# A fused linear-attention and gated-FFN kernel: its last stage put into a written order on all engines, small operands in PSUM, the first tiles' sums spread over the rounds before, and the output weights' splits gathered in one pass

## The chip, the cores and the metric

The kernel runs on one core of a Trainium2 chip. The metric is device time in microseconds (us). TensorE (PE) multiplies matrices from SBUF into PSUM, VectorE (DVE) and ScalarE (ACT) work on SBUF and PSUM, GpSimd (POOL) on SBUF, and SyncE (SP) issues every DMA. Each engine takes its instructions strictly in the order in which they were put into its queue; where an instruction waits for a semaphore, all behind it wait too.

## The reference

Sizes: S = 2048 tokens, D = 1024, 32 heads of 32, FF = 3584, all float32.

```python
xn = _layernorm(x, axis=-1)
# A: hedgehog linear attention, per head
pq, pk = q @ w_phi, k @ w_phi
phi_q = concat([softmax(pq), softmax(-pq)]); phi_k = concat([softmax(pk), softmax(-pk)])
kv = phi_k^T v ; z = sum(phi_k)
o = (phi_q kv) / (phi_q z + 1e-6)
s = o @ wo
# B: SwiGLU
g = _silu((_silu(xn @ w1) * (xn @ w3)) @ w2)
return x + s * g
```

## The kernel before

Each float32 operand of the large products is split into a high and a low float32r part (`split`: one ACT cast, one DVE subtraction), and a product is three passes over the parts (`PASSES`). The large products also use seven instead of eight block products (`ORDER`, `TURN`; the names A11, S2, T3 and so on are the sums and blocks of that scheme).

The program runs through five stretches. First layer norm and FFN's two up-products (L556), to 1184 us of the trace. Then three passes over eight pairs of token tiles (L639): pass c = 0 and c = 1 make keys and values (`heads`), pass c = 2 makes queries (`queries`) and stores for each of the 16 tiles `e`, two halves of 128x1024 exponentials, in DRAM. Between the products of the first two passes `split_wo` prepares the output weights `wo`: one block for each of the 16 pairs, loaded at step 0, split at step 3, stored at step 5 (L787 to L798). Each pair has seven steps, one per block product.

Then "down" (L913), from 1677 us: 7 blocks `kb` times 8 pairs `i`, a round per pair. A round is seven groups of six matmuls in the order S1, A11, S3, A12, S4, S2, A22 (`TURN`), three of them for the new pair (A11, A12, S2), the other four for the pair before. The groups of a pair share PSUM banks, so that S3 goes into the bank only after DVE has read S2 out of it, A22 after S3, S4 after S1. DVE adds the results into `acc` (L925); for A11, ACT copies (L922) and POOL adds (L923). In the last block (kb = 6) a finished pair is passed through SiLU (`gate`, L866) and stored to `g_d`, its `acc` buffers come free, and the loads of `e`, of `zb` (the sums z, spread to all partitions) and the output weights `wos` come in. The last, extra round has only S1, S3, S4, A22.

The last stage works tile by tile, 16 of them. `scales` turns e into weighted features: POOL multiplies e by zb into `ez` (L884), DVE sums e (L885) and ez (L887) over each head, six small operations of 128x32 give the factors `by` (L891 to L896), and both halves of e are multiplied by them, half 0 on DVE and half 1 on POOL (L899). `attend` transposes e on PE (`pt`, L1002), ACT copies it out (`et`, L1004), PE multiplies by kv (`po`, L1011), and `po` is split into `oT` (ACT L90, DVE L91). `output` multiplies oT by the output weights (`pm`, L99, 24 matmuls for each half of the columns), DVE multiplies by the gate (L1026), POOL adds x (L1027; DVE in the last tile), SP stores.

What sets the order: outside of `in_order(...)` a scheduler orders all engines' instructions by its own estimate; inside, the named engines keep the order in which the program writes them. Before the change, the last stage had SP, ACT, DVE and POOL in order for the extra round only, and SP alone for the first two tiles; for the rest the scheduler decided. `halves` and `output` are generators that interleave one tile's attention with the output product of the tile before.

Of the kernel before, what the change touches and what calls it, by code (L numbers as in the profile page):

```python
# [28 lines left out]
def tile_kernel(ctx: ExitStack, tc: tile.TileContext, x, wkT, wqT, wv, wphi, wo, w1, w3, w2, out):  # L29
# [757 lines left out]
    wso = []  # L787

    def split_wo(c, k, j):
        if j == 0:  # L790
            wso.append(work.tile([P, 512], F, name="wsr", tag="w"))
            nc.sync.dma_start(wso[-1], wo[k * P:(k + 1) * P, c * 512:(c + 1) * 512])
        elif j == 3:
            wso.append(quad("wso").rearrange("p u k t -> p u (k t)"))
            split(wso[1][:, 0], wso[1][:, 1], wso[0])
        elif j == 5:
            nc.sync.dma_start(wo_d[c][k], wso[1].bitcast(F))
            wso.clear()  # L798
# [8 lines left out]
    for c in range(3):  # L807
# [49 lines left out]
    wos, es = {}, {}  # L857
# [11 lines left out]
    E_TAGS = (0, 4, 1, 5, 2, 6)  # L869

    def load_e(i):

        two = []
        for c in range(2):
            two.append(accp.tile([P, 1024], F, name="e", tag=f"acc{E_TAGS[(2 * i + c) % 6]}"))
            nc.sync.dma_start(two[c], e_d[i][c])
        return two

    def scales(e):

        sums = small.tile([P, 2, 2, 16, 2], F, name="sums")
        for c in range(2):
            ez = accp.tile([P, 1024], F, name="ez", tag="accE", bufs=3)
            nc.gpsimd.tensor_mul(ez, e[c], zb[c])  # L884
            nc.vector.tensor_reduce(sums[:, 0, c].rearrange("p h s -> p (h s)"), e[c].rearrange("p (h f) -> p h f", f=DH),  # L885
                                    axis=AX.X, op=OP.add)
            nc.vector.tensor_reduce(sums[:, 1, c].rearrange("p h s -> p (h s)"), ez.rearrange("p (h f) -> p h f", f=DH),  # L887
                                    axis=AX.X, op=OP.add)
        by = small.tile([P, 2, 16, 2], F, name="by")
        t = small.tile([P, 2, 2, 16], F, name="rho")  # L890
        nc.vector.reciprocal(t[:, 0], sums[:, 0, :, :, 1])  # L891
        nc.vector.tensor_mul(t[:, 0], sums[:, 0, :, :, 0], t[:, 0])
        nc.vector.tensor_mul(t[:, 1], sums[:, 1, :, :, 1], t[:, 0])  # L893
        nc.vector.tensor_add(t[:, 1], t[:, 1], sums[:, 1, :, :, 0])  # L894
        nc.vector.reciprocal(by[:, :, :, 0], t[:, 1])  # L895
        nc.vector.tensor_mul(by[:, :, :, 1], by[:, :, :, 0], t[:, 0])  # L896
        for c, eng in enumerate((nc.vector, nc.gpsimd)):
            e3 = e[c].rearrange("p (h f) -> p h f", f=DH)
            eng.tensor_mul(e3, e3, by[:, c].rearrange("p h s -> p (h s)").unsqueeze(2).to_broadcast([P, H, DH]))  # L899
        return e  # L900
# [31 lines left out]
    for r, new in enumerate(steps):  # L932
# [32 lines left out]
        if end:  # L965
# [5 lines left out]
            if i == 3:  # L971
# [3 lines left out]
                es[0] = load_e(0)  # L975
            if i == 4:
# [12 lines left out]
    ps = pool("ps4", 3, space=PSUM)  # L989

    gate(*pairs[-1])
    in_order(ENG.SP)

    def attend(c, e):


        po = ps.tile([P, 2, 512], F, name="po", tag="po", bufs=1)
        ets = []
        for q in range(2):
            pt = ps.tile([P, 4, P], F, name="pt2", tag="tr", bufs=3)  # L1000
            for g in range(4):
                nc.tensor.transpose(pt[:, g, :], e[:, (4 * q + g) * P:(4 * q + g + 1) * P], ident)  # L1002
            et = work.tile([P, 4, P], F, name="et", tag="w")
            nc.scalar.copy(et, pt)  # L1004
            ets.append(et)
        yield
        for q, et in enumerate(ets):
            for g in range(4):
                for hh in range(2):
                    sl = slice(64 * hh, 64 * hh + 64)  # L1010
                    nc.tensor.matmul(po[32 * g:32 * g + 32, hh, q * P:(q + 1) * P], kvu[sl, G * c + 4 * q + g], et[sl, g],  # L1011
                                     start=True, stop=True, skip_group_check=True)
        oT = quad("oT")
        o4 = oT.rearrange("p u (h q) t -> p u h q t", q=2)
        split(o4[:, 0], o4[:, 1], po[:, :, :2 * P].rearrange("p h (q t) -> p h q t", t=P))
        yield oT

    def output(i, oT):
        for c in range(2):
            cs = slice(c * 512, c * 512 + 512)  # L1020
            gx = accp.tile([P, 2, 512], F, name="gx", tag="accZ", bufs=3)
            nc.sync.dma_start(gx[:, 0], g_d[i][:, cs])
            nc.sync.dma_start(gx[:, 1], x[i * P:(i + 1) * P, cs])
            for p in project([t[:, :, k] for t in oT for k in range(4)], lambda k, a: wos[c, k][:, a]):
                yield
# [69 lines left out]
```

## Time and profile before

| what | value |
|---|---|
| three runs | median 2488.62 us (2486.26 to 2493.84) |
| the profiled execution, its own time | 2484.93 us |
| its span, first to last instruction | 2483.1 us |
| granted TensorE clock, mean | 0.995 |
| PE busy | 96% of the span |
| DVE, ACT, POOL busy | 69%, 36%, 30% |
| DMA | mean 236 GB/s |

In rows of the timeline the columns are start (us from the span's start), duration (us), engine, source line, operation, output<-inputs, shapes, count, and in brackets how long the engine had sat idle before it and what released it. PE's matmul durations overlap: the distance between the starts of two groups is what counts (2.72 us for 12 matmuls of 128x512). Rows of the waits list total us, times and the longest. Rows of one line's instructions give min/median/max in ns.

### The profile page before, as it was taken

What the parts mean: (1) busy time and instruction counts of PE and PEld (TensorE: products, weight loads), DVE (VectorE), ACT (ScalarE), POOL (GpSimd) and SP (SyncE); (2) the same over time, 40 slices, a digit from 0 to 9 for tenths busy, and PEclk for the clock granted to TensorE, in tenths of its full rate; (3) what the DMA queues carried; (4) which work ended last, traced back from release to release, by engine and by line L of the source; (5) the groups of instructions that cost most, each with busy time, mean ns of one, the idle gap of its engine ahead of it and who ended that gap; (6) DMA issues with size and microseconds to landing.
All of it is one profiled execution on the core that took longest, in us unless ns stands there. A gap on an engine that the chain in (4) does not pass through costs nothing. (4 is left out here: it accounts for less than half of the span.)

```text
span 2483.1 us, 35840 instructions
## 1 busy us (share of the span) xinstructions
PE 2388.2 (96%) x13552; PEld 1950.1 (79%) x13552; DVE 1704.0 (69%) x2465; ACT 900.8 (36%) x1564; POOL 735.4 (30%) x513
## 2 busy tenths in 40 slices
PE   5999999999999999999999999899999999988999
PEld 5888877788777887878788788787888888866777
DVE  8656777774567777774566666566678878897773
ACT  6444544443344444542222122234322222332221
POOL 1233455553355555551000000000011111146662
PEclk9999999999999999999999999999999999999999
DMA  7566688866877777775988888986444244565553
GB/s 255 176 221 223 225 276 289 294 227 213 270 271 241 262 253 250 267 251 198 364 289 297 279 303 330 330 331 234 173 178 151 96 153 178 215 222 178 171 173 117
DMA packets 291196, 584.99 MB, mean 236 GB/s; under 512 B 25808, under 2 KB 140496, under 8 KB 288336
## 3 DMA queue, kind: packets, MB, share of 16 engines
q1 hardware_dynamic: 291024, 582.71, 67.6%
q8 instruction: 107, 1.75, 0.3%
q14 instruction: 65, 0.53, 0.1%
HBM read 377.88 MB, written 204.74 MB: 235 GB/s over the span
## 5 line engine op out<-in xcount | busy, mean ns | idle before, releaser
L91 DVE TENSOR_TENSOR bo<-rw,bo 128x512 fp32r<-128x512 f32 x336 | 295.8, 882 | 140.4 <-ACT bo L90 137.7
L923 POOL TENSOR_TENSOR acc<-acc,u 128x512 f32<-128x512 f32 x48 | 62.6, 1304 | 618.7 <-ACT u L922 370.6
L90 ACT CAST bo<-rw 128x512 fp32r<-128x512 f32 x336 | 205.6, 620 | 47.5 <-DMA wkv_d0T<-wkvo 5.0
L913 PE MATMUL bankb<-bo,as 128*128 128x512 f32 x816 | 201.6, 390 | 2.7 <-DVE acc L925 2.6
L268 POOL TENSOR_TENSOR rw<-rw,t 128x512 f32<-128x512 f32 x56 | 79.6, 1422 | 383.4 <-DVE bo L91 383.3
L99 PE MATMUL pm<-wos,oT 128*128 128x512 f32 x768 | 192.1, 400 | 0.0
L913 PEld LDWEIGHTS bankb<-bo,as 128*128 128x128 f32 x816 | 152.9, 188 | 35.7 <-DVE acc L925 4.0
L556 PE MATMUL bankb<-op1A,bo 128*128 128x512 f32 x672 | 160.4, 394 | 13.0 <-DVE u L584 9.7
L556 PE MATMUL bankb<-op0A,bo 128*128 128x512 f32 x672 | 160.0, 392 | 9.1 <-DVE u L584 8.8
L99 PEld LDWEIGHTS pm<-wos,oT 128*128 128x128 f32 x768 | 140.3, 189 | 33.1 <-issue 6.3
L556 PE MATMUL bankc<-op0S,bo 128*128 128x512 f32 x672 | 163.3, 391 | 2.2 <-ACT u L582 1.4
L556 PE MATMUL bankb<-op0S,bo 128*128 128x512 f32 x672 | 163.3, 392 | 2.2 <-ACT u L575 2.2
L556 PE MATMUL bankc<-op1S,bo 128*128 128x512 f32 x672 | 161.8, 390 | 2.4 <-ACT u L582 1.8
L556 PE MATMUL bankb<-op1S,bo 128*128 128x512 f32 x672 | 161.5, 389 | 0.0
L556 PEld LDWEIGHTS bankb<-op1A,bo 128*128 128x128 f32 x672 | 126.3, 189 | 44.2 <-DVE u L584 14.3
L556 PEld LDWEIGHTS bankb<-op0A,bo 128*128 128x128 f32 x672 | 125.1, 188 | 38.1 <-DVE u L584 12.0
L556 PEld LDWEIGHTS bankc<-op1S,bo 128*128 128x128 f32 x672 | 125.9, 188 | 29.8 <-ACT u L582 2.7
L556 PEld LDWEIGHTS bankc<-op0S,bo 128*128 128x128 f32 x672 | 125.2, 188 | 29.3 <-ACT u L582 2.2
L556 PEld LDWEIGHTS bankb<-op0S,bo 128*128 128x128 f32 x672 | 125.0, 188 | 29.3 <-ACT u L575 3.7
L913 PE MATMUL bankc<-bo,as 128*128 128x512 f32 x576 | 146.9, 390 | 1.2 <-DMA bo<-w_d0B 1.2
L556 PEld LDWEIGHTS bankb<-op1S,bo 128*128 128x128 f32 x672 | 126.0, 188 | 26.6 <-ACT u L575 0.5
L913 PEld LDWEIGHTS bankc<-bo,as 128*128 128x128 f32 x576 | 107.9, 188 | 24.6 <-DMA bo<-w_d0B 2.0
(222 smaller groups left out, 4722.1 us busy)
## 6 DMA issues: line engine op xcount, KB each, us to landing
rw<-in_w SPq DMA_DIRECT2D x112, 512.0 KB, 5.1
h_d<-h SPq DMA_DIRECT2D x112, 256.0 KB, 7.0
hr<-h_d SPq DMA_DIRECT2D x56, 512.0 KB, 3.5
xoS<-xo_d0S SPq DMA_DIRECT2D x48, 512.0 KB, 9.1
xoS<-xo_d1S SPq DMA_DIRECT2D x48, 512.0 KB, 5.7
xoA<-xo_d0A SPq DMA_DIRECT2D x36, 512.0 KB, 8.5
xoA<-xo_d1A SPq DMA_DIRECT2D x36, 512.0 KB, 6.2
e_d<-eq SPq DMA_DIRECT2D x32, 512.0 KB, 6.2
```

The lines of the kernel that those rows point to most:

```text
L90: nc.scalar.copy(hi, src)
L91: (by or nc.vector).tensor_sub(lo, src, hi.bitcast(F))
L99: nc.tensor.matmul(p, xT[dch][:, a], w(dch, b), start=n == 0, stop=n == 3 * ND - 1)
L268: nc.gpsimd.tensor_sub(b11, b22, t2)
L556: nc.tensor.matmul(bank[b], bo[bn][:, w, k], ao[an][:, u, k], start=first and n == 0, stop=LAST[b] == an and n == 11, skip_group_check=True)
L913: nc.tensor.matmul(bank[b], t[:, u, pos + k], bos[kb, bn, k][:, w], start=first and n == 0, stop=LAST[b] == an and n == 5, skip_group_chec ...
L923: nc.gpsimd.tensor_add(c, c, u)
```

## The change

Four things.

1. The last stage is put in a written order on all five engines until its end. A tile's loop now writes: transposes of tile i+1 (16 in a row), the result of tile i-1's second half, loads, the product ez of tile i+3, the output product of tile i's first half (24 in a row), sums and factors of tile i+2, `po` of tile i+1 (64 in a row) with its splits, the result of tile i's first half, the scaling of tile i+2, and the output product of tile i's second half. e is loaded four tiles ahead instead of three.
2. In this stage the small operands rho, den and a copy of the factors for half 0 lie in a PSUM bank (`stat`); the factors on DVE have one SBUF input each, and so has DVE's scaling of e.
3. For tiles 0 and 1 the products, sums, factors and scaling are written out over down's last rounds (i = 3 to 7) instead of in two calls at i = 5 and i = 7, with four of the six small operations on POOL; the ez of the first tiles use `acc` buffers that come free earlier. zb is loaded at i = 1, e of tile 0 at i = 2, of tiles 1 and 2 at i = 4.
4. `split_wo` does all 16 blocks in pass c = 0, one every two steps, in buffers of their own (two of the `big` tiles) instead of the `work` and `q` buffers.

The diff, cut:

```diff
-                    if c < 2:
-                        split_wo(c, i, j)
+                    if c == 0 and 4 <= 7 * i + j < 40:
+                        split_wo(7 * i + j - 4)
...
+    def split_wo(step):
+        if step == 0:
+            wso["room"] = [big.tile([P, 8, 512], F, name="room", tag=f"big{j}") for j in range(2)]
+        for m in range(16):
+            room, at_ = wso["room"][m % 4 // 2], 3 * (m % 2)
+            raw_w, two = room[:, at_], room[:, at_ + 1:at_ + 3].bitcast(R)
+            c, k = m // 8, m % 8
+            if step == 2 * m:
+                nc.sync.dma_start(raw_w, wo[k * P:(k + 1) * P, c * 512:(c + 1) * 512])
+            elif step == 2 * m + 3:
+                split(two[:, 0], two[:, 1], raw_w)
+            elif step == 2 * m + 5:
+                nc.sync.dma_start(wo_d[c][k], two.bitcast(F))
...
+    def weigh(i, c, tag="E"):
+        t = accp.tile([P, 1024], F, name="ez", tag=f"acc{tag}", bufs=3 if tag == "E" else 1)
+        nc.gpsimd.tensor_mul(t, es[i][c], zb[c])
+        ez[i, c] = t
+    def factors(i, eng, rho, den):
+        sm = sums.pop(i)
+        by[i] = small.tile([P, 2, 16, 2], F, name="by")
+        nc.vector.reciprocal(rho, sm[:, 0, :, :, 1])
+        eng.tensor_mul(rho, sm[:, 0, :, :, 0], rho)
+        eng.tensor_mul(den, sm[:, 1, :, :, 1], rho)
+        eng.tensor_add(den, sm[:, 1, :, :, 0], den)
+        nc.vector.reciprocal(by[i][:, :, :, 0], den)
+        eng.tensor_mul(by[i][:, :, :, 1], by[i][:, :, :, 0], rho)
...
-            if i == 5:
-                scales(es[0])
-                es[1] = load_e(1)
-            if i == 7:
-                scales(es[1])
-                es[2] = load_e(2)
+            elif i == 3:
+                weigh(0, 0, "1")
+                weigh(0, 1, "5")
+                add_up(0, 0)
+            elif i == 4:
+                add_up(0, 1)
+                factors_early(0)
...
+            elif i == 5:
+                scale(0, 0, nc.vector)
+                scale(0, 1, nc.gpsimd)
+                weigh(1, 0, "7")
+                add_up(1, 0)
+            elif i == 6:
+                weigh(1, 1)
+                add_up(1, 1)
+                factors_early(1)
+            elif i == 7:
+                scale(1, 0, nc.vector)
+                scale(1, 1, nc.gpsimd)
+                weigh(2, 0)
+                weigh(2, 1)
...
-    in_order(ENG.SP)
+    in_order(ENG.PE, ENG.SP, ENG.Activation, ENG.DVE, ENG.Pool)
+    load_e(3)
+    stat = ps.tile([P, 2, 256], F, name="stat", bufs=1)
+    po = ps.tile([P, 2, 2, 2, P], F, name="po", bufs=1)
...
     for i in range(NT):
...
+            ets = turned(es.pop(i + 1))
+        if p1 is not None:
+            result(i - 1, 1, p1)
...
+            weigh(i + 3, 0)
+        p0 = half_out(oT, 0)
+        if i + 2 < NT:
+            add_up(i + 2, 0)
+            add_up(i + 2, 1)
+            factors(i + 2, nc.vector, rho, den)
+        if i + 3 < NT:
+            weigh(i + 3, 1)
+        oT_next = heads_out(ets) if nxt else None
+        result(i, 0, p0)
...
+            nc.vector.tensor_copy(by0.rearrange("p c h -> p (c h)"), by[i + 2][:, 0].rearrange("p h s -> p (h s)"))
+            scale(i + 2, 0, nc.vector, by0.rearrange("p c h -> p (c h)").rearrange("p (h s) -> p h s", s=2))
+            scale(i + 2, 1, nc.gpsimd)
+        p1 = half_out(oT, 1)
```

PE, last stage, half a tile before (`pt` are transposes, `pm` the output product, `po` the product with kv):

```order
L1002 MATMUL pt_18726<-ident,e 128x128 x4
L1002 MATMUL pt_18733<-ident,e 128x128 x4
L99 MATMUL pm<-wos,oT 128x512 x12
L1011 MATMUL po<-et,kvu 32x128 x16
L99 MATMUL pm<-wos,oT 128x512 x12
```

and a whole tile now (a row of 32 `po` is 64 in the trace, as a row of 16 is 32 there):

```order
L1036 MATMUL pt_18769<-ident,e 128x128 x4
L1036 MATMUL pt_18776<-ident,e 128x128 x4
L1036 MATMUL pt_18783<-ident,e 128x128 x4
L1036 MATMUL pt_18790<-ident,e 128x128 x4
L1063 MATMUL pm<-wos,oT 128x512 x24
L1049 MATMUL po<-et,kvu 32x128 x32
L1063 MATMUL pm<-wos,oT 128x512 x24
```

The amount is the same, in twice as long pieces: four changes of kind for each tile instead of eight. All of a tile's transposes stand together, so that half 1 of e is wanted right behind half 0.

DVE, last stage, one tile before, from the factors on:

```order
L891 RECIPROCAL rho<-sums 128x32
L892 TENSOR_TENSOR rho<-sums,rho 128x32
L893 TENSOR_TENSOR rho<-sums,rho 128x32
L894 TENSOR_TENSOR rho<-rho,sums 128x32
L895 RECIPROCAL by<-rho 128x32
L896 TENSOR_TENSOR by<-by,rho 128x32
L899 TENSOR_TENSOR e<-e,by 128x1024
L91 TENSOR_TENSOR oT<-po,oT 128x512
L1026 TENSOR_TENSOR gx<-pm,gx 128x512
L91 TENSOR_TENSOR oT<-po,oT 128x512
```

and now (`stat` is the PSUM bank):

```order
L901 RECIPROCAL stat<-sums 128x32
L902 TENSOR_TENSOR stat<-sums,stat 128x32
L903 TENSOR_TENSOR stat<-sums,stat 128x32
L904 TENSOR_TENSOR stat<-sums,stat 128x32
L905 RECIPROCAL by<-stat 128x32
L906 TENSOR_TENSOR by<-by,stat 128x32
L91 TENSOR_TENSOR oT<-po,oT 128x512 x2
L1076 TENSOR_TENSOR gx<-pm,gx 128x512
L1111 COPY stat<-by 128x32
L912 TENSOR_TENSOR e<-e,stat 128x1024
```

Both subtractions of `oT` and the gate's product `gx` now stand before the scaling of e; POOL's addition of x to this gx stands in its queue before POOL's scaling of e.

POOL, end of down before (`acc10` and `acc11` are the A11 additions of rounds 6 and 7, each `ez` a product with zb):

```order
L923 TENSOR_TENSOR acc10_14656<-acc10_14656,u_18372 128x512
L884 TENSOR_TENSOR ez_18329<-e_18166,zb_18161 128x1024
L884 TENSOR_TENSOR ez_18504<-e_18343,zb_18160 128x1024
L884 TENSOR_TENSOR ez_18508<-e_18345,zb_18161 128x1024
L884 TENSOR_TENSOR ez_18645<-e_18522,zb_18160 128x1024
L899 TENSOR_TENSOR e_18166<-e_18166,by_18333 128x1024
L884 TENSOR_TENSOR ez_18649<-e_18524,zb_18161 128x1024
L923 TENSOR_TENSOR acc11_14729<-acc11_14729,u_18439 128x512
```

and now, between the same two additions:

```order
L939 TENSOR_TENSOR acc10_14626<-acc10_14626,u_18351 128x512
L886 TENSOR_TENSOR ez_18496<-e_18236,zb_17968 128x1024
L886 TENSOR_TENSOR ez_18498<-e_18238,zb_17969 128x1024
L902 TENSOR_TENSOR rho_18407<-sums_18323,rho_18407 128x32
L903 TENSOR_TENSOR rho_18407<-sums_18323,rho_18407 128x32
L904 TENSOR_TENSOR rho_18407<-sums_18323,rho_18407 128x32
L906 TENSOR_TENSOR by_18408<-by_18408,rho_18407 128x32
L912 TENSOR_TENSOR e_18234<-e_18234,by_18408 128x1024
L886 TENSOR_TENSOR ez_18656<-e_18546,zb_17968 128x1024
L939 TENSOR_TENSOR acc11_14699<-acc11_14699,u_18430 128x512
```

Tile 0 is done with by then (its rows stand rounds earlier); the two ez in front are tile 2's, and the four small operations behind them are tile 1's factors, for which DVE's second reciprocal of tile 1 waits.

More of the change, by code (lines that the diff above doesn't have):

```diff
@@ L785, in a_second @@
         return {"S1": (t1, 0), "A22": (t1, 2), "S3": (t2, 0), "S4": (t2, 2)}
[L787 to L798, printed above, removed]
+    wso = {}
+    def split_wo(step):
[11 more added lines that the diff above has]
+                nc.sync.dma_start(wo_d[c][k], two.bitcast(F))
     for d, b, t in hs:
@@ L855, in tile_kernel @@
         load_b(0, n)
-    wos, es = {}, {}
+    wos, es, ez, sums, by = {}, {}, {}, {}, {}
     def load_wo(k):
@@ L867, in gate @@
             nc.sync.dma_start(g_d[t], acc[t].rearrange("p c n -> p (c n)"))
[L869 removed]
+    E_TAGS = (("0", "4"), ("2", "6"), ("1", "5"), ("7", "W"))
     def load_e(i):
[L873 removed]
+        es[i] = []
         for c in range(2):
[L875 to L885, printed above, removed]
[L886 to L900 removed]
@@ L1013, in attend @@
[L1013 to L1025, printed above, removed]
-            nc.vector.tensor_mul(gx[:, 0], p, gx[:, 0])
-            (nc.vector if i + 1 == NT else nc.gpsimd).tensor_add(gx[:, 0], gx[:, 0], gx[:, 1])
-            nc.sync.dma_start(out[i * P:(i + 1) * P, cs], gx[:, 0])
-        yield
@@ L1031, in halves, with heads_out @@
-    def halves(e):
+                nc.tensor.transpose(pt[:, g, :], e[m // 2][:, (4 * (m % 2) + g) * P:(4 * (m % 2) + g + 1) * P], ident)
+            ets.append(work.tile([P, 4, P], F, name="et", tag="w"))
+            nc.scalar.copy(ets[m], pt)
+        return ets
+    def heads_out(ets):
         oT = []
         for c in range(2):
-            a = attend(c, e[c])
-            next(a)
-            yield oT
-            oT.append(next(a))
-            yield oT
-    for oT in halves(es[0]):
-        pass
```

96 lines of the change are left out of this document (68 added, 28 removed).

## The prediction

> **What bounds the kernel now.** The page first, then PE's list of waits, then PE's timeline from down to the end.
>
> ```profile
> PE 2388.2 (96%) x13552; PEld 1950.1 (79%) x13552; DVE 1704.0 (69%) x2465; ACT 900.8 (36%) x1564; POOL 735.4 (30%) x513
> ```
> ```profile
> PE po L1011 <- DVE oT L91: 13.6, 9, 6.9
> PE bankb L639 <- DMA xoA<-xo_d0A: 9.5, 3, 6.6
> PE bankb L913 <- DVE acc L925: 5.0, 4, 1.9
> PE bankc L913 <- DVE acc L925: 3.9, 2, 2.9
> ```
>
> PE bounds the kernel as a whole, so only its gaps can be won. Of those in reach of the change, the last stage waits 13.6 us for DVE's `oT`, down 8.9 us for DVE's reads, the head passes 9.5 us for DMA. The windows say where.
>
> ```profile
> 2200.00:2220.00 20.00, 15.53 (x65) 11.55 (x63) 18.55 (x18) 3.69 (x5) 18.43 (x8) 1.00 0.44 153
> 2260.00:2280.00 20.00, 16.60 (x139) 12.86 (x137) 17.08 (x21) 3.62 (x7) 14.49 (x7) 0.99 0.58 184
> ```
>
> At 2200 (down's end) DVE and POOL are full (18.55 and 18.43 of 20 us) and PE is not (15.53). PE's groups give the bill:
>
> ```profile
> 2187.26 1.52 PE L913 MATMUL bankc<-bo,as 128*128 128x512 f32 x6
> 2188.62 1.52 PE L913 MATMUL bankb<-bo,af 128*128 128x512 f32 x6
> ...
> 2230.88 1.66 PE L913 MATMUL bankb<-bo,as 128*128 128x512 f32 x6 [1.48 <-DVE acc L925]
> 2233.32 1.53 PE L1002 MATMUL pt<-ident,e 128*128 128x128 f32 x12 [0.79 <-DVE acc L925]
> ...
> 2283.52 1.11 PE L1011 MATMUL po<-et,kvu 64*32 64x128 f32 x32 [6.92 <-DVE oT L91]
> ...
> 2449.74 0.67 PE L1011 MATMUL po<-et,kvu 64*32 64x128 f32 x32
> 2450.33 3.02 PE L99 MATMUL pm<-wos,oT 128*128 128x512 f32 x12
> 2453.19 1.03 PE L1002 MATMUL pt<-ident,e 128*128 128x128 f32 x8
> 2453.98 2.98 PE L99 MATMUL pm<-wos,oT 128*128 128x512 f32 x12
> 2456.89 0.67 PE L1011 MATMUL po<-et,kvu 64*32 64x128 f32 x32
> ...
> 2464.64 13.89 PE L99 MATMUL pm<-wos,oT 128*128 128x512 f32 x60
> ```
>
> Six matmuls take 1.36 us from start to start, a round of seven groups 9.52. From 2187.26 two rounds end at 2206.3, and 11 more groups (round 7 and the extra round) at 2221.3. Before ends 2230.88 + 1.36 = 2232.24: **10.9 us lost at down's end**. The last stage runs from there to 2464.64 + 60 x 0.2267 = 2478.24: **246.0 us**. Without waits half a tile takes 2456.89 - 2449.74 = 7.15, so 16 tiles 228.8: 17 us lost there, by the 6.92 us wait and by this, in each tile:
>
> ```profile
> 2336.62 0.67 PE L1011 MATMUL po<-et,kvu 64*32 64x128 f32 x32
> 2337.40 0.59 ACT L90 CAST oT<-po 128x512 fp32r<-128x512 f32 x1 [2.71 <-PE po L1011]
> 2338.72 0.63 DVE L1026 TENSOR_TENSOR gx<-pm,gx 128x512 f32<-128x512 f32 x1
> 2339.43 1.29 POOL L1027 TENSOR_TENSOR gx<-gx 128x512 f32<-128x512 f32 x1 [2.14 <-DVE gx L1026]
> 2341.64 1.22 DVE L899 TENSOR_TENSOR e<-e,by 128x1024 f32<-128x1024 f32 x1
> 2341.77 2.86 POOL L899 TENSOR_TENSOR e<-e,by 128x1024 f32<-128x1024 f32 x1 [1.06 <-DVE by L896]
> 2344.60 2.38 POOL L884 TENSOR_TENSOR ez<-e,zb 128x1024 f32<-128x1024 f32 x1
> 2344.74 0.67 PE L1011 MATMUL po<-et,kvu 64*32 64x128 f32 x32 [0.89 <-DVE oT L91]
> 2360.00 0.67 PE L1011 MATMUL po<-et,kvu 64*32 64x128 f32 x32 [0.87 <-DVE oT L91]
> ```
>
> The same wait comes 15.26 us later: a ring of ez (POOL), sums and factors (DVE) and scaling (POOL, DVE) sets the pace, 0.96 us over PE's 14.30.
>
> **The last stage's loop.** Where DVE's two inputs both lie in SBUF it is held up beside POOL; with one input in PSUM it is not:
>
> ```profile
> L893 DVE TENSOR_TENSOR rho<-sums,rho x16: 181/1281/1901, 2208.8 to 2431.1; 128x32 f32<-128x32 f32 x16
> ```
> ```profile
> L899 POOL TENSOR_TENSOR e<-e,by x16: 1915/2864/2917, 2215.4 to 2433.4; 128x1024 f32<-128x1024 f32 x16
> ```
> ```profile
> L91 DVE TENSOR_TENSOR oT<-po,oT x32: 673/681/694, 2236.5 to 2465.4; 128x512 fp32r<-128x512 f32 x32
> ```
> ```profile
> L1026 DVE TENSOR_TENSOR gx<-pm,gx x32: 627/681/693, 2244.4 to 2478.6; 128x512 f32<-128x512 f32 x32
> ```
>
> `rho` takes 0.18 us alone, 1.28 usually; POOL's scaling 1.92 alone, 2.86 beside DVE's. All 64 operations with a PSUM input stay under 0.70. So I take 1.92 for POOL's scaling, 2.86 as the other end. The Trainium skill, SBUF — State Buffer, section Who interferes with whom, says that a DVE instruction with at most one SBUF input does not contend with GpSimd: by that rule the loop is the 14.40 us worked out below, without it 15.34; no run here shows it for the operations that were moved.
>
> PE's own time for a tile: two halves less one pair of changes of kind. The 12 pm before pt take 2.86 and before po 2.91, against 2.72 pure: 0.33. 14.30 - 0.33 = 13.97.
>
> DVE per tile: four sums at 1.21 (line 885 has 31.4 us for 26, below), six small ones (4 x 0.19 + 2 x 0.35 = 1.5), two oT and two gx at 0.68, a copy of at most 0.35, e 1.22: some 10.6. POOL: 2 x 1.29 + 2 x 2.38 + 1.92 = 9.3. Both are under 14, so the sums, one tile further ahead now, hide.
>
> ```profile
> L885 DVE TENSOR_REDUCE sums<-e 128x32 f32<-128x1024 f32 x26 | 31.4, 1209 | 4.9 <-DMA e<-e_d 4.7
> ```
>
> A shorter ring is left, made by the written order: half 1 of e of tile i+2 is scaled only after POOL's add, that after DVE's gx, that after both oT, and PE wants it behind four groups' transposes. From the end of po: 0.18 to ACT (2337.40 less 2336.62 + 0.60), cast 0.59, oT 0.69, cast 0.59, oT 0.69 (one after the other, since the second cast waits for the first subtraction), three hand-overs of 0.04: 2.86; gx 0.60, hand-over 0.08, add 1.25 (start to start), scaling 1.92: 6.71; to PE 0.1. Then eight transposes 0.79, 24 pm 5.63, 64 po 1.18: 14.40. That is 0.43 over 13.97, in 14 tiles: 6.0 us.
>
> Start of the stage: 1.08 us from down's end to pt, as before (2233.32 - 2232.24). ACT's last SiLU stands ahead of the copies as before, first copy after 2.0, fourth done at 4.2, po done at 4.5, the serial casts and oT 2.86, the next tile's fourth transposes after them: pm starts at 7.7. From there 16 x 48 x 0.2267 = 174.1, 15 po at 1.18 + 0.19, 14 x 16 transposes at 1.58 + 0.14: 218.8. Stage: 7.7 + 218.8 + 6.0 = **232.5, 13.5 less** than 246.0. The end behind PE (DVE, store) is unchanged. SP's queue: a store of half a tile stands ahead of e (four tiles ahead) and gx (half a tile ahead); 2.5 MB a tile as before, so nothing is late.
>
> **Down's end.** DVE's work for tiles 0 and 1 stays (eight sums, four reciprocals, two scalings), but starts in round 3, since ez uses buffers that are free then; the small products go to POOL. What remains is POOL's queue in round 6.
>
> ```profile
> 2200.12 2.73 POOL L884 TENSOR_TENSOR ez<-e,zb 128x1024 f32<-128x1024 f32 x1 [7.47 <-ACT acc L866]
> ```
> ```profile
> g_d<-acc SPq DMA_DIRECT2D x16, 512.0 KB, 2.9
> ```
> ```profile
> 2196.30 1.06 ACT L866 ACTIVATE acc<-acc 128x1024 f32<-128x1024 f32 x1 [2.07 <-DVE acc L925]
> ```
>
> Tile 1's second ez still waits for acc8: S4 of round 5 read at 2195.0, SiLU 1.06, store 2.9: 2199.2; ez 2.38, A11's add 1.29, tile 2's two ez 4.8, three small products: 2208.5. A small one I put at 0.26 (an estimate: 1.29 at 512 elements and 2.38 at 1024 give 2.1 ns an element), with 1.29 as the upper end. DVE's second reciprocal waits for them, and behind it stands S2's read: done at 2210, where PE's S3 wants it at 2206.3 + 2.72 = 2209.0. About 1.3 us, and 0.5 for DVE's scaling beside POOL: 1.8 of 10.9 remain, **9.1 less**. With 1.29 for the small ones 3.1 more remain.
>
> **The splits of wo.** Counted: 16 loads, casts, subtractions, stores before and now.
>
> ```profile
> 1386.85 0.38 SPq L797 DMA_DIRECT2D wo_d<-wso  x1
> 1390.27 0.85 SPq L521 DMA_DIRECT2D xoA<-xo_d0A  x2
> ```
> ```profile
> 1397.92 2.35 PE L639 MATMUL bankb<-op3B,xoA 128*128 128x512 f32 x9 [1.51 <-DMA xoA<-xo_d0A]
> ```
>
> In pass 1 a store and a load stood for 3.4 us on SP ahead of xoA, and PE waited 1.51: **1.5 less**. The 6.6 us wait is in pass 2, where the order is the same: 0. In pass 0 the work doubles:
>
> ```profile
> 1220.00:1240.00 20.00, 20.00 (x206) 16.46 (x192) 13.15 (x18) 4.45 (x7) 0.26 (x2) 1.00 1.00 368
> ```
> ```profile
> 1223.71 0.62 ACT L90 CAST wso<-wsr 128x512 fp32r<-128x512 f32 x1 [2.49 <-DMA wsr<-in_wo]
> ```
>
> DVE's 13.15 of 20 us get 2.5 x 0.6 a pair, ACT's 4.45 as much: hidden under PE. But DMA is at 1.00 there, and a cast waits for its load with ACT's copies for PE behind it (2.49 us here): 0 taken, the bad end is a rival.
>
> **Sum**: 13.5 + 9.1 + 1.5 = 24.1; on the execution's own 2484.93 that is 2460.8. The runs' median is 3.7 above it: **2464.5 us**. 0.3% is 7.5 us, about what a measurement of this kernel can tell from no change.
>
> **Rivals.**
> - *The operands in PSUM do not free POOL.* Its scaling stays at 2.86, the ring at 15.34: 0.94 x 14 = 13.2 back, 2477.7. Against it the 64 rows under 0.70. 0.08; half of it within 0.3%, if down gains less too.
> - *Down's end stays late*: POOL's small products or the ez before them take so long that DVE's reads come as late as before: 9.1 back, 2473.6. For it, DVE's wait at the head of its queue. 0.12.
> - *The short ring does not bind* (PE's weights load ahead of the wait): 6.0 more, 2458.5. 0.08.
> - *Slower: casts of wo hold ACT in pass 0.* A bank must be read within one group (2.72 us less the copy's 0.59, so 2.1); a load that comes 4.5 us after ACT reaches its cast costs PE 2.4, sixteen of them 38: 2464.5 + 38 = 2503. Slower from 2.0 us each on. For it DMA at 1.00; against it, SP issues a load three steps (8 us) before its split, and PE waited nowhere in that window. 0.06.
>
> The forecast has 0.66. **Faster** 0.66 + 0.04 + 0.12 + 0.08 = 0.90, **same** 0.04, **slower** 0.06. The range holds the forecast with its bounds (small products, start of the stage: 2458 to 2470), the ring that does not bind, and the first two rivals: 2455 to 2479.
>
> **What would show it.** Right: down's last group ends near 2223 (pass 1's 1.5 us moves all times), pm steadily 14.4 us a tile, POOL's e at 1.92 in every tile, PE's pt waiting 0.2 to 0.5 us for POOL's e. Wrong: POOL's e at 2.86; gaps of PE in pass 0 behind ACT's copies; a period of 15 us or more; PE waiting over 3 us for `acc` at down's end.

## The result, and the profile after

| | before | changed |
|---|---|---|
| median of the runs, us (lowest to highest) | 2486.10 (2484.32 to 2493.84, 6 runs) | 2472.86 (2465.74 to 2478.22, 6 runs) |
| the profiled execution's own time, us | 2484.93 | 2471.39 |
| its span, us | 2483.1 | 2469.6 |

The changed kernel takes 0.9943 of the time before (95% interval 0.9921 to 0.9964): it is faster by 13 to 14 us, where 24 were forecast. To see where, cut each profiled execution at the first PE group of each stage (for down at its second group, since the matmuls of the first stand among the last of pass 2). The cuts of the changed kernel, in PE's timeline:

```profile
1181.64 2.88 PE L639 MATMUL bankb<-op2B,xoA 128*128 128x512 f32 x12
...
1351.05 3.00 PE L639 MATMUL bankb<-op3B,xoA 128*128 128x512 f32 x12
...
1526.41 3.00 PE L639 MATMUL bankb<-op4B,xoA 128*128 128x512 f32 x12
...
1688.16 1.52 PE L929 MATMUL banka<-bo,af 128*128 128x512 f32 x6
...
2233.14 1.53 PE L929 MATMUL bankb<-bo,as 128*128 128x512 f32 x6
2234.51 1.47 PE L1036 MATMUL pt<-ident,e 128*128 128x128 f32 x12
...
2241.92 5.71 PE L1063 MATMUL pm<-wos,oT 128*128 128x512 f32 x24
...
2448.39 16.63 PE L1063 MATMUL pm<-wos,oT 128*128 128x512 f32 x72
```

The first four rows begin head passes 0, 1 and 2 and down; the fifth plus 1.36 us is down's end, 2234.50; the last plus 72 x 0.2267 us is PE's end, 2464.7. The same cuts of all runs (each from one execution; the stages of a run add up to its own time):

| us | FFN | pass 0 | pass 1 | pass 2 | down | last stage | tail | median of the runs | ratio to before |
|---|---|---|---|---|---|---|---|---|---|
| before | 1184.0 | 170.6 | 168.4 | 164.4 | 544.8 | 246.0 | 6.7 | 2486.10 | |
| **changed** | 1181.6 | 169.4 | 175.4 | 161.8 | 546.3 | 230.2 | 6.7 | 2472.86 | 0.9943 (0.9921 to 0.9964) |
| e1 wo as before | 1179.7 | 170.7 | 170.4 | 165.0 | 547.9 | 230.3 | 6.7 | 2471.87 | 0.9940 (0.9924 to 0.9955) |
| e2 before, wo moved | 1180.8 | 170.0 | 175.5 | 162.3 | 545.9 | 245.5 | 6.7 | 2486.13 | 0.9992 (0.9979 to 1.0005) |
| e3 scaling first | 1181.4 | 170.8 | 177.5 | 161.6 | 546.0 | 227.7 | 6.7 | 2472.32 | 0.9935 (0.9916 to 0.9954) |
| e4 operands in SBUF | 1179.2 | 170.7 | 176.1 | 162.0 | 548.8 | 242.9 | 6.7 | 2486.10 | 0.9994 (0.9983 to 1.0005) |
| e5 POOL's order | 1181.1 | 170.0 | 173.6 | 162.5 | 541.1 | 230.3 | 6.7 | 2464.22 | 0.9919 (0.9900 to 0.9938) |
| e6 no weighing | 1185.4 | 170.1 | 176.3 | 161.9 | 536.3 | 230.4 | 6.7 | 2464.57 | 0.9915 (0.9901 to 0.9930) |
| e7 products on DVE | 1180.0 | 171.0 | 174.6 | 161.4 | 542.0 | 230.4 | 6.7 | 2468.88 | 0.9938 (0.9926 to 0.9951) |
| e8 stores on POOL | 1180.8 | 170.5 | 170.6 | 162.3 | 546.3 | 230.3 | 6.7 | 2467.53 | 0.9928 (0.9916 to 0.9940) |
| e9 e3 + e5 + e8 | 1180.0 | 170.2 | 173.2 | 162.8 | 540.0 | 227.5 | 6.7 | 2461.01 | 0.9903 (0.9881 to 0.9925) |
| e10 sums as before | 1182.3 | 170.7 | 174.7 | 161.3 | 549.9 | 230.3 | 6.7 | 2475.13 | 0.9961 (0.9947 to 0.9975) |
| e11 e4 + scaling first | 1179.1 | 170.8 | 176.3 | 162.3 | 547.3 | 227.5 | 6.7 | 2471.67 | 0.9945 (0.9928 to 0.9962) |

From before to changed: FFN -2.4, passes -1.2, +7.0 and -2.6, down +1.5, last stage -15.8: -13.5 in all. No line of the FFN was touched, and it ranges from 1179.1 to 1185.4 us over these runs: its 2.4 us is scatter. What the table is good for are the stages that repeat: the last stage is 230.2 to 230.4 us in every run that leaves it as changed, and down 546.0 to 548.8 in the six that leave down as changed (e1, e3, e4, e8, e11 and the changed kernel itself). The ratios are each against the runs of before on the same chip, whose medians lie between 2485.3 and 2488.0. One of e10's nine executions took 4195.63 us, at a granted clock of 0.68; the row's median and ratio are those of the other eight.

The page's first line and PE's list of waits:

```profile
PE 2385.4 (97%) x13552; PEld 1954.8 (79%) x13552; DVE 1686.7 (68%) x2471; ACT 901.4 (36%) x1564; POOL 726.3 (29%) x521
```
```profile
PE bankb L639 <- DMA xoA<-xo_d0A: 11.6, 4, 5.2
PE bankb L929 <- DVE acc L941: 6.2, 4, 2.5
PE bankc L929 <- DVE acc L941: 3.3, 1, 3.3
```

The last stage's 13.6 us of waits for `oT` are gone. Down's waits for DVE's reads are not: 6.2 + 3.3 = 9.5 us where there were 8.9. Nor are the waits for xoA, 11.6 where there were 9.5.

**The last stage did what the prediction said.** One line's durations, and PE's weight loads' list of waits for 2245 to 2460:

```profile
L912 POOL TENSOR_TENSOR e<-e,by x16: 1912/1922/1926, 2187.3 to 2438.8; 128x1024 f32<-128x1024 f32 x16
```
```profile
PEld pt L1036 <- POOL e L912: 4.2, 14, 0.3
```

POOL's scaling takes 1.92 us in all sixteen tiles (2.86 before), and the wait that is left is the forecast one, 0.30 us a tile.

**Down's end did not.** PE's timeline there, then POOL's and DVE's:

```profile
2210.19 1.66 PE L929 MATMUL bankb<-bo,as 128*128 128x512 f32 x6 [2.10 <-DVE acc L941]
...
2217.11 1.61 PE L929 MATMUL bankb<-late,as 128*128 128x512 f32 x6 [2.54 <-DVE acc L941]
...
2223.39 2.92 PE L929 MATMUL bankc<-late,as 128*128 128x512 f32 x6 [3.31 <-DVE acc L941]
```
```profile
2203.53 2.56 POOL L886 TENSOR_TENSOR ez<-e,zb 128x1024 f32<-128x1024 f32 x1 [3.24 <-issue]
2206.06 1.46 POOL L939 TENSOR_TENSOR acc<-acc,u 128x512 f32<-128x512 f32 x1
2209.62 5.21 POOL L886 TENSOR_TENSOR ez<-e,zb 128x1024 f32<-128x1024 f32 x2 [2.10 <-DVE sums L894]
2214.78 0.27 POOL L902 TENSOR_TENSOR rho<-sums,rho 128x32 f32<-128x32 f32 x1
...
2216.55 1.92 POOL L912 TENSOR_TENSOR e<-e,by 128x1024 f32<-128x1024 f32 x1
2218.43 2.56 POOL L886 TENSOR_TENSOR ez<-e,zb 128x1024 f32<-128x1024 f32 x1
```
```profile
2204.36 2.02 DVE L780 TENSOR_TENSOR s<-hr,sm 128x256 f32<-128x256 f32 x1
2206.30 1.51 DVE L781 TENSOR_TENSOR s<-hr,sm 128x256 f32<-128x256 f32 x1
...
2210.06 2.50 DVE L91 TENSOR_TENSOR as<-s,as 128x512 fp32r<-128x512 f32 x1
...
2215.74 0.35 DVE L905 RECIPROCAL by<-rho 128x32 f32<-128x32 f32 x1 [1.77 <-POOL rho L904]
...
2216.88 1.87 DVE L781 TENSOR_TENSOR s<-hr,sm 128x256 f32<-128x256 f32 x1
2218.68 2.86 DVE L91 TENSOR_TENSOR as<-hr,as 128x512 fp32r<-128x512 f32 x1
```

POOL and DVE wait for each other here in both ways. In queue order: tile 2's weighing at 2209.62 waits for DVE's sums, tile 1's small products stand behind that weighing, and DVE's second reciprocal waits for them, with a bank's read behind it. And while POOL weighs (2203.5 to 2206.1, 2209.6 to 2214.8, 2218.4 to 2221.0), adds (2206.1 to 2207.5) or scales (2216.6 to 2218.5), DVE's differences and splits, which have two SBUF inputs, take 1.5 to 2.9 us; the same operations take 0.41 (`s`) and 0.68 (`as`) beside an idle POOL (the rows of e6 below).

### The profile page after: what moved, and what is told of

It reads as the page before. It is cut to its first block, busy times and chain, and to the rows that moved or that the text cites. A ratio compares the mean times of both kernels' runs of the same rounds, so it can differ in the third digit from the quotient of the medians.

```text
span 2469.6 us, 35815 instructions
## 1 busy us (share of the span) xinstructions
PE 2385.4 (97%) x13552; PEld 1954.8 (79%) x13552; DVE 1686.7 (68%) x2471; ACT 901.4 (36%) x1564; POOL 726.3 (29%) x521
## 3 DMA queue, kind: packets, MB, share of 16 engines
q8 instruction: 107, 1.75, 0.3%
## 4 chain that ended last, share of the span: by engine, by line
PE 69%; DMA 11%; DVE 7%; issue 6%; POOL 4%; SPq 1%; ACT 1%; DVEq 0%; ACTq 0%; POOLq 0%
PE bankb L556 18%; PE bankb L929 11%; PE bankb L639 9%; PE bankc L556 8%; PE bankc L929 6%; PE banka L556 4%; PE bankc L639 4%; PE banka L929 3%; PE banka L639 2%; POOL ez L886 2%; PE pm L1063 2%; DVE bo L91 2%; DMA xoA<-xo_d0A 1%; POOL e L912 1%; DMA wkv_d0T<-wkvo 1%
## 5 line engine op out<-in xcount | busy, mean ns | idle before, releaser
L1063 PE MATMUL pm<-wos,oT 128*128 128x512 f32 x768 | 182.9, 394 | 0.0
L556 PE MATMUL bankb<-op1A,bo 128*128 128x512 f32 x672 | 161.3, 396 | 11.7 <-DVE u L584 8.5
L556 PE MATMUL bankc<-op1S,bo 128*128 128x512 f32 x672 | 161.8, 390 | 3.1 <-ACT u L582 1.9
```

Source lines behind the costliest of these rows:

```text
L556: nc.tensor.matmul(bank[b], bo[bn][:, w, k], ao[an][:, u, k], start=first and n == 0, stop=LAST[b] == an and n == 11, skip_group_check=True)
L1063: nc.tensor.matmul(p, oT[k // 4][:, a, k % 4], wos[c, k][:, b], start=n == 0, stop=n == 23)
```

## The experiments

### What the last stage owes to what (e3, e4, e11)

e4 puts the quotients back into SBUF and leaves the written order:

```
-        st = stat[:, i % 2]
-        rho, den, by0 = (st[:, a:a + 32]. ...)
+        t = small.tile([P, 2, 2, 16], F, name="rho")
+        rho, den = t[:, 0], t[:, 1]
...
-            nc.vector.tensor_copy(by0 ..., by[i + 2][:, 0] ...)
-            scale(i + 2, 0, nc.vector, by0 ...)
+            scale(i + 2, 0, nc.vector)
```

> The changed kernel with the quotients of the last stage in SBUF (the small products have two SBUF inputs, DVE's scaling too; the copy of by goes). Theory (an operand in PSUM frees DVE and POOL of each other): POOL's scaling takes 2.86 instead of 1.92 us and the ring 0.94 a tile more, 13.2 in 14 tiles, 2486; where the small products are held too (1.28 instead of 0.20 us beside POOL's ez), DVE is 2 us a tile later and the time up to 2512. Rival (the written order alone makes the stage, the place of the operands does nothing): 2473, POOL's scaling at 1.92.

Measured: 2486.10, no faster than before; last stage 242.9, 12.7 us longer than changed. The number is the one expected, the reason is not. (From 246.0 before to 242.9: this written order with the operands in SBUF gives 3.1 of the 15.8 us.) Durations by line, and four rows of one tile:

```profile
L912 POOL TENSOR_TENSOR e<-e,by x16: 1911/1912/1916, 2189.5 to 2453.9; 128x1024 f32<-128x1024 f32 x16
```
```profile
L902 DVE TENSOR_TENSOR rho<-sums,rho x14: 193/2182/2240, 2248.9 to 2444.5; 128x32 f32<-128x32 f32 x14
```
```profile
2330.19 1.22 DVE L912 TENSOR_TENSOR e<-e,by 128x1024 f32<-128x1024 f32 x1
2330.35 2.20 POOL L1076 TENSOR_TENSOR gx<-gx 128x512 f32<-128x512 f32 x1 [5.14 <-DVE gx L1075]
...
2332.51 1.91 POOL L912 TENSOR_TENSOR e<-e,by 128x1024 f32<-128x1024 f32 x1
```
```profile
2334.48 1.09 PE L1035 MATMUL pt<-ident,e 128*128 128x128 f32 x8 [0.94 <-POOL e L912]
```

POOL's scaling is still 1.91 us. What is held is POOL's addition, which in this order stands ahead of it and now runs beside DVE's scaling with two SBUF inputs: 2.20 us instead of 1.29. Those 0.91 us are in the ring; PE waits 0.94 in each of 14 tiles, 13.2 us. DVE's first small product is held too (2.18 us, 0.196 with the operand in PSUM), but DVE has the time. That the kernel's time fits the expectation is chance: 0.91 us on the addition is nearly the 0.94 that was expected on the scaling.

e3 keeps PSUM and moves POOL's scaling ahead of the additions:

```
+        if i + 2 < NT:
+            scale(i + 2, 1, nc.gpsimd)
         result(i, 0, p0)
...
-            scale(i + 2, 1, nc.gpsimd)
```

> The changed kernel with POOL's scaling of e for the tile after next ahead of DVE's multiplication and POOL's addition of result(i, 0). Theory (the short ring binds: weight loads for the third transposes wait 0.30 us a tile for POOL's e): the wait goes, a tile takes 13.97 instead of 14.26 us, 14 tiles 4.1 us, 2468.8. Rival (PE's own transposes and changes of kind make the 14.26): same, 2472.9, and the third group of transposes still waits or the time shows in other groups.

Measured: last stage 227.7, 2.5 us less, and no weight load waits for POOL's e. The median is 2472.32; a gain of 2.5 us is below what the ratios can tell, and in the profiled execution pass 1 took 2.1 of it back. PE's timeline gives the tile:

```profile
2313.38 1.98 PE L1036 MATMUL pt<-ident,e 128*128 128x128 f32 x16
...
2327.47 1.98 PE L1036 MATMUL pt<-ident,e 128*128 128x128 f32 x16
```

14.09 us instead of 14.26 (2439.67 less 2425.41 in the changed kernel), and 16 transposes in 1.74 from start to start (2329.21 less 2327.47) instead of 1.94: this is PE's own pace, 0.12 above the 13.97 that the prediction worked out; the ring cost 0.17 a tile, not 0.43. So theory and rival each have a part: of the 0.29 between 14.26 and 13.97, the short ring makes 0.17 and PE's own work 0.12.

e11 does both, operands in SBUF and the scaling ahead:

> The kernel of the run with the quotients in SBUF, with POOL's scaling also moved ahead of the additions. In that run POOL's scaling was not slower (1.91 us); POOL's addition beside DVE's scaling was (2.20 instead of 1.30), and it stood ahead of POOL's scaling. Theory (the operand in PSUM pays only because the addition is in the ring): with the scaling ahead of it the last stage takes 228 to 231 us, as with the operands in PSUM, and the kernel 2470 to 2473. Rival (the held products and scaling cost DVE or POOL elsewhere in the tile, 2 us and more): the last stage stays above 238 us, 2480 or more.

Measured: last stage 227.5, kernel 2471.67. The held operations are still there (`rho` 1.33 us in the median, an addition up to 2.21), but none of them stands between one matmul and the next. So in this stage the operands in PSUM are worth 12.7 us in one order and nothing in the other: it is the order that decides whether contention costs time.

### Down's end (e5, e6, e7, e10)

e5 fixes POOL's order from the round of tile pair 6 on:

```
+        if end and i == 6:
+            in_order(ENG.Pool)
         if new is None:
             in_order(ENG.SP, ENG.Activation, ENG.DVE, ENG.Pool)
```

> The changed kernel with POOL's order fixed from the last tile pair but one of down: tile 1's small products come ahead of tile 2's two weighings, and the last addition into acc ahead of the scaling of tile 1. Theory 1 (DVE's second reciprocal stands behind POOL's products, these behind 5.2 us of tile 2's weighing that in turn waited 2.1 us for DVE's sums, and DVE's reads of the banks behind the reciprocal): the products come about 5 us earlier, PE's waits at down's end fall from 9.5 to about 4.5 us, the kernel from 2472.9 to 2468. Theory 2 (DVE is held by POOL's work wherever that stands, since its splits and differences have two SBUF inputs): the waits move and stay above 8 us, 2471.5 to 2473.

Measured: down 541.1, 5.2 less than changed, kernel 2464.22. POOL's and PE's timelines:

```profile
2205.52 2.58 POOL L886 TENSOR_TENSOR ez<-e,zb 128x1024 f32<-128x1024 f32 x1
2208.99 0.57 POOL L902 TENSOR_TENSOR rho<-sums,rho 128x32 f32<-128x32 f32 x1 [0.89 <-DVE rho L901]
...
2216.87 1.66 POOL L939 TENSOR_TENSOR acc<-acc,u 128x512 f32<-128x512 f32 x1 [3.85 <-ACT u L938]
...
2220.36 7.11 POOL L886 TENSOR_TENSOR ez<-e,zb 128x1024 f32<-128x1024 f32 x3
```
```profile
2210.11 2.22 PE L929 MATMUL bankb<-bo,as 128*128 128x512 f32 x6 [2.38 <-DVE acc L941]
...
2228.19 1.47 PE L1038 MATMUL pt<-ident,e 128*128 128x128 f32 x12
```

The products start at 2208.99 instead of 2214.78, and the last two waits (2.54 and 3.31 us) are gone; PE's wait for DVE falls from 9.5 to 4.1 us, as theory 1 expected; theory 2's 8 us is not seen. Three weighings now lie behind DVE's last split. Both parts of what theory 1 and theory 2 name moved at once, so this run alone doesn't divide the 5.2 us between them.

e6 takes the four weighings of tiles 1 and 2 out of down:

```
-                weigh(1, 0, "7")
+                ez[1, 0] = es[1][0]
...
-                weigh(1, 1)
+                ez[1, 1] = es[1][1]
...
-                weigh(2, 0)
-                weigh(2, 1)
+                ez[2, 0], ez[2, 1] = es[2]
```

> The changed kernel without the four weighings of tiles 1 and 2 on POOL in down; the sums that would read them read e instead, so that DVE has as many sums as before and the outputs of tiles 1 and 2 are scaled with other quotients. Theory 1 and 2 together (POOL's weighing, as work that DVE waits for and as work that holds DVE's instructions): down's end loses at most 2.5 of the 9.5 us, 2466. Rival (DVE's own load, eight sums of 1.2 us and the rest, makes its reads late): 8 us and more remain, 2472.

Measured: down 536.3, 10.0 us less. DVE has all its sums, and PE waits for it 2.4 us. DVE's timeline, the operations that were held in the changed kernel:

```profile
2206.15 0.41 DVE L780 TENSOR_TENSOR s<-hr,sm 128x256 f32<-128x256 f32 x1
...
2207.09 0.41 DVE L781 TENSOR_TENSOR s<-hr,sm 128x256 f32<-128x256 f32 x1
2207.42 0.68 DVE L91 TENSOR_TENSOR as<-hr,as 128x512 fp32r<-128x512 f32 x1
```

Two operations are still held there: an `as` of 1.44 us at 2209.75, beside the one weighing that is left (tile 3's), and an `s` of 1.88 at 2215.94, beside POOL's scaling. So it is not DVE's load: POOL's weighing, as a queue and as company, costs 10 us at down's end, 546.3 less 536.3.

e7 gives the small products of tiles 0 and 1 back to DVE:

```
-        factors(i, nc.gpsimd, t[:, 0], t[:, 1])
+        factors(i, nc.vector, t[:, 0], t[:, 1])
```

> The changed kernel with the small products of tiles 0 and 1 back on DVE. Theory 1 (the hand-over to POOL costs: 1.77 us of waiting in front of the reciprocal and 5 us of weighing before it): PE's waits at down's end fall to 5 us or less, 2468.5. Theory 2 (DVE is held beside POOL): the four products take up to 1.3 us each there instead of 0.2, and the waits stay near 9.5, 2472.9.

Measured: down 542.0, PE's waits 6.3 us, between the two and nearer to theory 1. The hand-over to POOL cost about 4 us; of the four products that DVE does instead for tile 1, one is held for long, here beside POOL's weighing:

```profile
2215.59 2.23 DVE L904 TENSOR_TENSOR rho<-sums,rho 128x32 f32<-128x32 f32 x1
```

e10 puts the sums back where they were, under the new last stage:

```
-            if i == 1:
+            if i == 3:
                 zb = ...
+                load_e(0)
...
+            elif i in (5, 7):
+                m = (i - 5) // 2
+                for c in range(2):
+                    weigh(m, c)
+                    add_up(m, c)
+                factors_early(m)
+                scale(m, 0, nc.vector)
+                scale(m, 1, nc.gpsimd)
+                load_e(m + 1)
```

with the products on DVE, and `weigh(2, 0)`, `weigh(2, 1)` at the head of the last stage.

> The changed kernel with the sums of tiles 0 and 1 back where they were (all of a tile's in one round, tile 0 in the sixth, tile 1 in the eighth, small products on DVE; tile 2's weighing opens the last stage). Theory (the changed kernel's spreading gave nothing: down took 546.3 us there and 544.8 before): down 544 to 546 us, the last stage as now or up to 3 us longer, since tile 1's scaling ends about 4 us behind down's end; 2470 to 2476. What the prediction held (the spreading takes 9 us off down's end): 2480 or more.

Measured: down 549.9, the kernel 2475.1. Neither number: 4 us more in down than the theory expected, much less than the prediction's 9. So the changed kernel's spreading does save, but only 1 to 4 us (549.9 less the 546.0 to 548.8 of the runs that leave down as changed). e10 has the small products on DVE, though. The run that spreads the sums and has the products there too is e7, and against its 542.0 the spreading (with its earlier loads) saves 7.9 us; the hand-over of the products to POOL gives back about 4 of them. Under the new last stage down starts from 549.9 and not from 544.8. POOL's timelines, before and in e10, whose down begins 1.5 us later:

```profile
2204.61 7.09 POOL L884 TENSOR_TENSOR ez<-e,zb 128x1024 f32<-128x1024 f32 x3
...
2220.62 1.29 POOL L923 TENSOR_TENSOR acc<-acc,u 128x512 f32<-128x512 f32 x1
```
```profile
2208.76 7.06 POOL L886 TENSOR_TENSOR ez<-e,zb 128x1024 f32<-128x1024 f32 x3 [1.76 <-DVE sums L894]
...
2219.93 5.72 POOL L886 TENSOR_TENSOR ez<-e,zb 128x1024 f32<-128x1024 f32 x2
2225.61 1.29 POOL L939 TENSOR_TENSOR acc<-acc,u 128x512 f32<-128x512 f32 x1
```

Counted from down's start, the last addition into `acc` begins 3.5 us later than before. Tile 2's weighing stands ahead of it, but it did so before the change too. The queue is late earlier on: the three weighings begin 2.6 us later, behind a wait of 1.76 us for DVE's sums. DVE waits 3.55 us for the late addition (at 2226.93), and PE 4.98 us for DVE's reads (at 2232.42). That this is the whole difference between 549.9 and 544.8 is argued, not tried by itself.

### The head passes (e1, e2, e8)

e1 is the changed kernel with `split_wo` and its calls as before; e2 is the kernel before with the new `split_wo` alone. The calls in e1 (in e2 the other way round):

```
-                    if c == 0 and 4 <= 7 * i + j < 40:
-                        split_wo(7 * i + j - 4)
+                    if c < 2:
+                        split_wo(c, i, j)
```

> The changed kernel with the splits of wo as they were before (one load, split and store a round in passes 0 and 1). In the profile of the changed kernel pass 1 was 6.9 us longer than before, and PE waited 5.16 us for xoA at its head where it had waited 1.51. Theory A (moving the splits, and the op3B loads behind them, makes xoA late): the wait goes back to about 1.5 us and the kernel gains about 5 us on the changed kernel's 2472.9, 2468. Theory B (the sixteen small stores of kv_out hold SP's queue whatever the splits do, and the wait differs from run to run): within 2 us of 2472.9, the wait anywhere from 1.5 to 6 us. Theory C (the splits are worth the 1.5 us that the prediction gave them): 2474.4.

> The kernel before with only the splits of wo moved to pass 0. Theory A: about 5 us slower than before, 2491. Theory B: within 2 us of 2486.1. Theory C: 2484.6. By all three the last stage stays 246 us and down's end as before.

Measured: 2471.87 against 2472.86, and 2486.13 against 2486.10: for the time as a whole the splits do nothing that these runs can tell. Theory A is right on the wait and wrong on the time. At the head of pass 1 PE waits 1.51 and 1.88 us for xoA in the two runs that leave the splits (before and e1), and 4.05 to 7.47 in the nine that move them and keep the small stores on SP; theory B's scatter from run to run doesn't make two such groups. In pass 2 it is the other way, 6.61 and 7.07 against 4.08 to 5.60. So pass 1 is 173.6 to 177.5 us in those nine and 168.4 and 170.4 in the two, and pass 2 gives 2 to 4 us back (161.3 to 162.5 against 164.4 and 165.0). The row that the prediction spoke of, in e1 and in the changed kernel, and SP's queue ahead of it in the changed kernel:

```profile
1394.06 4.61 PE L639 MATMUL bankb<-op3B,xoA 128*128 128x512 f32 x12 [1.88 <-DMA xoA<-xo_d0A]
```
```profile
1398.92 5.33 PE L639 MATMUL bankb<-op3B,xoA 128*128 128x512 f32 x12 [5.16 <-DMA xoA<-xo_d0A]
```
```profile
1368.87 0.32 SPq L735 DMA_DIRECT2D kv_d<-kva  x1
...
1385.68 4.04 SPq L736 DMA_DIRECT2D z_d<-zs  x1
1389.82 0.85 SPq L521 DMA_DIRECT2D xoA<-xo_d0A  x2
```

The store and load of wo are gone from the queue, and xoA is issued 1389.82 - 1351.05 = 38.8 us into the pass; before, with them, it was 35.6 (1390.27 - 1354.63). `kv_out`'s sixteen small stores hold SP either way, but not for as long: 20.9 us (1368.87 to 1389.7) against 14.6 before (1372.15 to 1386.75).

e8 issues those stores on POOL's queue:

```
-                nc.sync.dma_start(kv_d[j % 2, ...], ...)
-                nc.sync.dma_start(z_d[0, c, :, j, s]..., ...)
+                nc.gpsimd.dma_start(kv_d[j % 2, ...], ...)
+                nc.gpsimd.dma_start(z_d[0, c, :, j, s]..., ...)
```

> The changed kernel with the sixteen small stores of kv_out issued on POOL's queue instead of SP's. POOL has nothing to do in these passes. Theory (the stores hold SP: xoA is issued 38.8 us after the pass's first op3B group, behind stores that each wait for an earlier transfer): xoA is issued 15 us or more earlier, the two waits at the heads of passes 1 and 2 (5.2 and 4.1 us, and 2.3 us of lowered clock behind each) go, 2459. Rival (xoA then waits for its buffer, or the DMA engines are full there): at most 3 us, 2470.

Measured: pass 1 170.6, 4.8 less, the kernel 2467.53, between the theory's 2459 and the rival's 2470. That the stores on SP's queue make xoA late in pass 1 is shown by this: the two loads issued at 1389.82 and 1390.29 in the changed kernel are issued at 1371.25 and 1375.73, and the longest wait left in pass 1 is 1.42 us. In pass 2 the wait only changed its name: PE waits 5.24 us for DVE, and DVE 12.06 for the stores of e to land. POOL's queue issues the small stores at the same time (1534.56 to 1555.05); that they delay those of e is not shown.

```profile
1561.73 0.69 DVE L688 TENSOR_TENSOR eq<-k,mm 128x512 f32<-128x512 f32 x1 [12.06 <-DMA e_d<-eq]
```

### Together (e9)

> The changed kernel with three of the edits tried apart: POOL's scaling ahead of the additions in the last stage, POOL's order fixed in down, kv_out's stores on POOL's queue. If they are independent, their stages add: 2.5 us in the last stage, 5.2 in down and 4.8 in pass 1 off the changed kernel's own 2471.4, 2459. If the wait at a pass's head only moves elsewhere: 2462 to 2465.

Measured: 2461.01 in the median, 0.9903 (0.9881 to 0.9925) of before, some 24 us less. The profiled execution's own time is 2460.5: the last stage (227.5) and down (540.0) add up as expected, pass 1 (173.2) keeps only 2.2 of e8's 4.8. PE no longer waits for xoA in that pass, but it waits 3.87 us for a weight block (op3T), where it waited 0.86 in e8. So in pass 1 the gain of the stores on POOL is seen in one execution, e8's, and 173.2 is hardly below the 173.6 of e5.

## Why the prediction came out as it did

Direction and range held; the size was little over half. The range held because it had been drawn to take in the first two rivals: 2472.86 lies outside the 2458 to 2470 that the forecast's own bounds gave. By its terms:

- **Last stage**, forecast 232.5 (13.5 less): 230.2 (15.8 less). The start, 7.7 forecast, took 2241.92 - 2234.50 = 7.4. A tile, 14.40 forecast, took 14.26: the serial casts, the addition ahead of the scaling and PE's wait on the third transposes are all there, but 0.12 of the excess was PE's own pace. POOL's scaling was 1.92, as taken. The reason given for it was too narrow: e4 shows that the price of operands in SBUF sits in POOL's addition, not in the scaling, and e11 that another order makes it nothing. The rule that was cited (the Trainium skill, SBUF — State Buffer, section Who interferes with whom) is borne out: a tile's first product takes 0.196 us with one input in PSUM and, beside POOL's weighing, 2.18 with both in SBUF (e4, median of 14).
- **Down's end**, forecast 9.1 less: 1.5 more. This is the step that failed, "What remains is POOL's queue in round 6". That queue was forecast to be through with the small products at 2208.5; they ended at 2215.7. The second weighing of tile 1 began at 2203.53 instead of 2199.2, since the read of `acc` that it waits for stood behind sums and a scaling on DVE. Tile 2's weighing then waited 2.10 us for DVE's sums, a wait that the forecast lacks. And the five held operations of DVE shown above (2.02, 1.51, 2.50, 2.86 and an `s` of 1.87 us at 2216.88) cost 10.76 - 2.59 = 8.2 us over their free time, where 0.5 had been allowed: the rule used for the last stage was not applied to DVE's splits. DVE had been held at down's end before, too (2.67, 1.81, 1.75 and 2.55 us for operations that take 0.68, 0.18, 0.18 and 1.21 alone, 6.5 over), and the forecast let nearly all of that go with the spreading. The spreading was not the mistake by itself: with the products on DVE it saves 7.9 us (e7 against e10), though e7's down is only 2.8 below before's. The sign of being wrong that the prediction named, PE waiting over 3 us for `acc`, is there. This is the second rival, priced at 2473.6 and given a chance of 0.12. That the median, 2472.86, comes so near to its price is luck in part: the last stage gave 2.3 us more than forecast, and the FFN and the head passes together took 0.8 us more where 1.5 less were forecast.
- **The splits of wo**, forecast 1.5 less: nothing measurable in the whole time, and the wait itself rose from 1.51 to 5.16 us. It was not what two transfers cost on SP but what sixteen small stores do, and with the splits moved these held SP 6 us longer. The rival of ACT's casts did not happen: PE waited nowhere in pass 0 behind them, and that pass is 169.4 to 171.0 us in all runs.
- The 2.6 us in pass 2 and the scatter of the FFN were in no term.

What stays open: why xoA is issued later in pass 1 with the splits moved, and how e5's 5.2 us divide between queue order and held DVE instructions. On the first the traces go one step further. The stores begin as late after the pass's start as before, but two of them wait, 2.75 and 4.04 us, until 1383.25 and 1389.72. Just before, two packets of the DMA queues that the trace calls `instruction` end: 8 KB from 1379.66 to 1383.11, and 16 KB from 1385.61 to 1389.39. The same stands in all nine runs that move the splits and keep the stores on SP (two waits of 1.65 to 4.04 us, each ending 0.1 to 0.4 us behind such a packet of 1.7 to 3.8 us). In before and e1 no store waits over a microsecond, and the packet that falls among the stores takes 0.88 us. That the one causes the other was not tried.

## What to carry to other kernels

Before work is spread over "free" rounds of another stage, ask of each operation there which of its partners it will run beside: two engines that hold each other up lose more than the queue shows, and the victim can be an instruction that the change never touched. Check an engine's queue for waits in both directions, since a queue worked out alone (POOL's here) lacks the waits for the other's results. And where contention can't be avoided, order the queue so that the held operation is not between two steps of the bound engine: here that was worth as much as moving the operands.

## What the hardware showed beside this

- A wait of PE's has a second price when it is long. After 1.51 us (before, pass 1) the next group of twelve took 3.04 us; after 5.16 and 4.12 us (changed, passes 1 and 2) it took 5.33 and 5.22, with a granted clock of 0.66 in the 10 us from 1396. The Trainium skill, TensorE: Matmul & The Clock Gate, section HAM oscillation — how this bites in real kernels, warns of idle gaps of PE above about 3.4 us; these three waits agree. So do all waits of 3.87 us and more in the head passes of the thirteen kernels: the next group took 4.34 to 5.49 us. Below that bound the runs go both ways, and there the measurement decides: e1's wait of 1.88 us in pass 1 was followed by a group of 4.61 (its row stands above; granted clock 0.66 in the 5 us from 1394), a wait of 1.91 us in e6's pass 0 by one of 3.01. Before, 0.51, 0.88 and 1.42 us of waiting within 6.1 us were followed by a group of 4.57 us, while 0.88, 1.43 and 0.86 us in the changed kernel were not (3.04). What decides between them is not shown.
- A busy share of the DMA engines can come from few packets that take long. The changed kernel's window behind the small stores in pass 1 (the last two columns are the share, by the packets that begin in the window, and GB/s) shows 0.90 at 40 GB/s:

```profile
1388.00:1392.00 4.00, 4.00 (x20) 3.30 (x18) 1.12 (x2) 0.00 (x0) 0.00 (x0) 1.00 0.90 40
```

The small stores don't make it: 162 packets of 4 and 128 bytes begin in this window and have 0.02 of the share. The rest is 39 packets of 4 KB that begin behind the issue of xoA, from 1390.83 on; the median one takes 0.18 us, twelve take 2.1 to 5.5. While the small stores were being issued, from 1374 to 1384, the share was 0.29.
